# A global spectral filter and a squared-ReLU FFN on one core: the stages B and Y of each batch moved by a slot

## The chip, the cores and the metric

The kernel runs on one core of one Trainium2 chip, in one launch. The metric is the device time of that launch in microseconds; six runs of the kernel before are given.

A core has TensorE (PE, with its weight loads PEld), VectorE (DVE), ScalarE (ACT), GpSimd (POOL) and SyncE (SP). Matmuls write to PSUM, DVE and ACT read it and write to SBUF. Nearly all transfers of this kernel are issued from SP, in program order. Every engine takes its own instructions in the order in which the program gives them, and waits where an input or a buffer is not ready.

## The reference

Eight batches of 3008 positions and 256 channels are filtered in the frequency domain along the positions, and the result goes through a feed-forward layer token by token:

```python
X = np.fft.rfft(x, axis=1)                       # x: (8, 3008, 256)
Y = X * (filt_r + 1j * filt_i)[None, :, :]       # 1505 frequencies
y = np.fft.irfft(Y, n=3008, axis=1)
h = np.maximum(y.reshape(24064, 256) @ w_in, 0)  # w_in: (256, 2048)
return h * h @ w_out                             # w_out: (2048, 256)
```

Inputs and output are float32; the kernel computes with float16 operands and float32 accumulation.

## The kernel before, in words

**The feed-forward layer** sets the frame. The 24064 tokens are 47 groups of 512, and each group has 8 slots, so there are 47 x 8 slots, and 8 more at the end (line 731). In slot s, with g = s // 8 and k = s % 8, the program issues in this order:

1. `ffn_g1(g, k)` (L560): four matmuls of 512 columns, which give two of the sixteen 128-row tiles of the hidden layer into one of two psH buffers, and ACT's ReLU of them into `h` (L564). A group that spans two batches has more and narrower matmuls.
2. place 0 of the slot: what the plan of the filter puts there.
3. `ffn_g2(g - 1, k)` (L577): eight matmuls of 256 columns on the previous group's `h` into psO. `h` is the stationary operand. For even k they read hidden tiles 0 to 7, which are those of that group's slots 0 to 3, for odd k tiles 8 to 15, those of its slots 4 to 7.
4. place 1 of the slot.
5. `ffn_out`: in every fourth slot (s % 4 == 3) ACT copies psO out (L588) and SP writes it to the output (L603, L605).
6. `ffn_sq(g, k)` (L568): DVE squares what ACT wrote in step 1.

**The filter** of batch b is a two-step Fourier transform, its product and its inverse, spread over the slots of earlier groups so that the batch is ready when its tokens come up. Its units:

- A (16 units, `unit_a`, L346): one matmul of 512 columns into psF, copied by ACT (even) or DVE (odd); each fourth is followed by a write of the chunk to `dU` in DRAM. DVE casts x beforehand (`cast_x`, L338), 4 per batch, from loads of x (`load_x`, L192), two of which wait for the buffers that the first two casts free.
- the read of `dU` back in another layout, in two DMAs (`read_u`, L434) into the single tile `ut`.
- B (12 units, `unit_b`, L437): two matmuls of 256 columns into psF (L443). On DVE the product with the filter (L451, "product" below) and two copies across partition halves (L458, L459), and then, as unit S, the sum (L465), which leaves `yf`.
- P (12 units, `unit_p`): two matmuls of 256 columns from `yf` into psF (L494), copied by ACT (L496). After P 2, 5, 8 and 11 SP writes a part of `dZ` to DRAM (L499).
- the read of `dZ` in a third layout, eight DMAs of 192 KB into four tiles `zt` (`read_z`, L512).
- Y (16 units, `unit_y`, L516): four matmuls of 94 columns from `zt` into psF (L530), copied into the batch's `yt` by ACT for even and by DVE for odd units (L537, L539); the last four of batch 0 all by ACT. `ffn_g1` reads `yt`. Units 0 to 3 give the first 752 tokens of the batch, units 4 to 7 the next 752.

`psF` has two buffers (L157), which go round through all of A, B, P and Y in program order: a unit waits until the unit two before it has been emptied.

The order is written out by hand. `fft_plan(b)` (L608) gives each unit a slot and a place, in slots relative to the batch; `first` (L727) turns them into slots of the program: 0 for batch 1, and 40, 88, 136, 184, 232, 280 for batches 2 to 7. All of these are multiples of 8, so that relative slots 24, 32, 40 and 48 of every batch begin a group. Batch b's first tokens are in the group that begins in relative slot 48 (40 for batch 1). Batch 0, and most of A of batch 1, are done before the slots, and Y 4 to 15 of batch 0 in slots 4 to 23 (L616). A unit S is put beside its B, and a P two slots after its B, in place 1. Relative slots before:

| unit | batch 1 | batches 2 to 7 |
|---|---|---|
| A | 8, 9 (last four) | 6 to 13 |
| read_u | 10 | 14 |
| B 0 to 11 | 14 15 17 18 20 22 23 25 27 28 30 32 | 18 19 21 23 24 26 28 30 31 33 35 37 |
| load_x 0, 1 of the next batch | 22 | 27 |
| cast_x 0 to 3 of the next batch (load_x 2, 3 after the first two) | 27 30 33 36 | 32 35 38 41 |
| read_z | 35 | 40 |
| Y | 39 (four), 40 to 45 (two each) | 44 to 51 (two each) |
| Y 12 to 15 of batch 0 | 17 19 21 23 | |

Of the kernel before, what the change touches and what calls it, by code (L numbers as in the profile page):

```python
# [110 lines left out]
def kernel(  # L111
# [496 lines left out]
    def fft_plan(b):  # L608

        plan = {}  # L610

        def put(r, place, f, *a):
            plan.setdefault((r, place), []).append((f, a))

        if b == 1:
            for n in range(4, 16):  # L616
                put(n if n < 8 else n + 2 if n < 12 else 2 * n - 7, n % 2, unit_y, 0, n)
            for k in range(4):
                put((4, 5, 7, 7)[k], 1, cast_wout, k, nc.vector)
        t0 = 2 if b == 1 else 6  # L620
        for a in range(12 if b == 1 else 0, 16):
            put(t0 + a // 2, a % 2, unit_a, b, a)
        put(10 if b == 1 else 14, 1, read_u, b)
        t0 = 14 if b == 1 else 18
        for p in range(12):
            r = t0 + (18 if b == 1 else 19) * p // 11
            put(r, 0, unit_b, b, p)
            put(r, 0, unit_s, b, p)
            put(r + 2, 1, unit_p, b, p)
        t0 = 35 if b == 1 else 40  # L630
        for c in range(4):
            put(t0, 1, read_z, b, c)
        if b + 1 < B:
            for c in range(2):
                put(t0 - 13, 1, load_x, b + 1, c)
            for c in range(4):
                r = t0 - 8 + 3 * c
                put(r, 1, cast_x, b + 1, c)
                if c < 2:
                    put(r, 1, load_x, b + 1, c + 2)  # L640
        for n in range(16):
            if b == 1:
                put(38 + n // 2 if n > 3 else 39, n % 2, unit_y, b, n)
            else:
                put(44 + n // 2, n % 2, unit_y, b, n)
        return plan

    def run(plan, r, place):
# [77 lines left out]
    for b in range(1, B):  # L726
        first = (b * S // TG) * SLOTS - (48 if b > 1 else 40)  # L727
        for (r, place), w in fft_plan(b).items():
            work[(first + r, place)] = w
# [43 lines left out]
```

## Time and profile before

| | |
|---|---|
| six runs | 795.63 to 798.05 us, median 796.97 |
| the profiled execution | 798.05 us; its span, first to last instruction, is 796.2 |
| granted clock of TensorE | 0.998 of full speed |
| first slot begins | 51.5 us into the span |
| bytes read and written in HBM | 58.12 and 48.23 MB, 134 GB/s over the span |

Times in the views are microseconds from the start of the span. A row of the timeline is one operation of one engine or several of a kind: start, length, engine, line, operation, what it writes and reads with the tile's names, the shapes, how many; in brackets the idle time of that engine before it and what ended it. The matmuls' starts are measured, their ends are modelled: a matmul of 256 columns is shown as 272 ns long, while one starts every 109 ns. A row of the view of waits gives the engine, tile and line that waited, what ended the wait, the total, how often, and the longest. The chain that ended last is followed back from the last instruction, and gives the share of the span that each engine has in it.

### The profile page before, as it was taken

How to read it: one execution, taken by the hardware profiler on the slowest of the kernel's cores; microseconds unless marked ns; L12 is line 12 of the kernel's file. 1: busy time of each engine (PE TensorE's matmuls, PEld its weight loads, DVE VectorE, ACT ScalarE, POOL GpSimd, SP SyncE). 2: the span in 40 equal slices, each digit the busy share in tenths (PEclk: the TensorE clock that was granted, in tenths of full speed). 3: DMA queues.
4: the chain of work that ended last, by engine and by line, in shares of the span. 5: the costliest groups of instructions: out<-in, count | busy, mean ns of one | idle time of the engine just before them, and what ended most of it. 6: DMA issues, size and time to landing. Idle time of an engine off the chain costs nothing.

```text
span 796.2 us, 14801 instructions
## 1 busy us (share of the span) xinstructions
PE 781.4 (98%) x6102; PEld 553.2 (69%) x6102; DVE 552.4 (69%) x898; ACT 555.0 (70%) x708; POOL 24.3 (3%) x27
## 2 busy tenths in 40 slices
PE   8989999999999999999999999999999999999998
PEld 5746767666676677867778676776767667776666
DVE  6946995579755897559965699557995579554342
ACT  3856776767667677767777677676777767766664
POOL 3710000000000000000000000000000000000000
PEclk9999999999999999999999999999999999999999
DMA  9994555346814567055461555525563342511111
GB/s 350 366 264 143 138 157 130 88 137 160 202 53 107 154 167 183 28 162 157 121 183 48 169 156 134 132 68 158 151 175 97 86 141 80 122 50 41 40 41 54
DMA packets 88139, 107.32 MB, mean 135 GB/s; under 512 B 6288, under 2 KB 78864, under 8 KB 83856
## 3 DMA queue, kind: packets, MB, share of 16 engines
q1 hardware_dynamic: 87864, 106.19, 46.9%
q8 instruction: 48, 0.79, 0.4%
q10 hardware_dynamic: 144, 0.18, 0.1%
q14 instruction: 19, 0.16, 0.1%
q0 software_dynamic: 64, 0.00, 0.0%
HBM read 58.12 MB, written 48.23 MB: 134 GB/s over the span
## 4 chain that ended last, share of the span: by engine, by line
PE 93%; DMA 4%; DVE 1%; ACT 1%; issue 0%; SPq 0%; ACTq 0%; DVEq 0%
PE psO L577 40%; PE psH L560 39%; PE psB L443 3%; PE psA L359 3%; PE psY L530 3%; PE psP L494 2%; DMA zt<-dZ 1%; DMA ut<-dU 1%; PE warm L274 1%; DMA dZ<-ze 1%; PE psf L293 1%; PE psf L296 1%; ACT h L564 1%; DMA dU<-u 0%; PE psP L480 0%; PE psT L420 0%
## 5 line engine op out<-in xcount | busy, mean ns | idle before, releaser
L564 ACT ACTIVATE h<-psH 128x1024 f16<-128x1024 f32 x376 | 385.2, 1025 | 190.5 <-PE psH L560 187.6
L577 PE MATMUL psO<-sWout,h 128*128 128x256 f16 x3008 | 388.6, 272 | 0.0
L560 PE MATMUL psH<-yt,sWin 128*128 128x512 f16 (+7 forms) x1728 | 386.9, 351 | 1.8 <-DVE yt L539 0.8
L577 PEld LDWEIGHTS <-h 128*128 128x128 f16 x3008 | 290.6, 98 | 77.2
L568 DVE TENSOR_TENSOR h<-h 128x1024 f16<-128x1024 f16 x376 | 253.8, 685 | 100.7 <-ACT h L564 99.2
L560 PEld LDWEIGHTS <-sWin 128*128 128x128 f16 x1728 | 159.5, 98 | 101.7 <-issue 3.5
L451 DVE TENSOR_TENSOR prod<-psB,sF 128x1024 f16<-128x1024 f32 x84 | 102.5, 1220 | 6.3 <-PE psB L443 6.0
L539 DVE CAST yt<-psY 128x376 f16<-128x376 f32 x62 | 34.0, 550 | 58.3 <-PE psY L530 58.3
L365 DVE CAST u<-psA 96x512 f16<-96x512 f32 x50 | 34.3, 687 | 47.3 <-PE psA L359 45.1
L496 ACT CAST ze<-psP 128x512 f16<-128x512 f32 x84 | 49.2, 586 | 17.8 <-PE psP L494 15.9
L588 ACT COPY ost<-psO 128x512 f32<-128x512 f32 (+1 forms) x96 | 55.7, 580 | 6.7 <-PE psO L577 5.3
L530 PEld LDWEIGHTS <-zt 112*128 112x128 f16 x512 | 34.9, 98 | 13.1 <-issue 3.2
L530 PE MATMUL psY<-sC,zt 112*128 112x94 f16 x512 | 42.3, 205 | 1.5 <-DMA zt<-dZ 1.2
L465 DVE TENSOR_TENSOR yf<-prod,yf 128x512 f16<-128x512 f16 x84 | 35.7, 425 | 2.9
L443 PE MATMUL psB<-ut,sSB 128*128 128x256 f16 x192 | 36.5, 272 | 0.7 <-DMA ut<-dU 0.6
L359 PE MATMUL psA<-x,sC 94*96 94x512 f16 x96 | 36.6, 382 | 0.0
L443 PEld LDWEIGHTS <-sSB 128*128 128x128 f16 x192 | 18.6, 98 | 21.3 <-issue 2.1
L494 PE MATMUL psP<-yf,sSP 128*128 128x256 f16 x168 | 32.1, 273 | 0.2 <-ACT yt L537 0.2
L537 ACT CAST yt<-psY 128x376 f16<-128x376 f32 x66 | 30.8, 468 | 1.6 <-PE psY L530 1.0
L338 DVE CAST x<-x 94x2048 f16<-94x2048 f32 x24 | 29.2, 1216 | 0.0
L363 ACT CAST u<-psA 96x512 f16<-96x512 f32 x50 | 28.6, 572 | 0.0
L458 DVE COPY yf<-prod 64x512 f16<-64x512 f16 x84 | 24.3, 290 | 2.9
(63 smaller groups left out, 253.1 us busy)
## 6 DMA issues: line engine op xcount, KB each, us to landing
x<-in_x_dram SPq DMA_DIRECT2D x20, 768.0 KB
zt<-dZ SPq DMA_DIRECT2D x64, 192.0 KB
dU<-u SPq DMA_DIRECT2D x28, 384.0 KB
dZ<-ze SPq DMA_DIRECT2D x28, 384.0 KB
out_dram<-ost SPq DMA_DIRECT2D x66, 128.0 KB
out_dram<-ost SPq DMA_DIRECT2D x31, 256.0 KB
ut<-dU SPq DMA_DIRECT2D x7, 1024.0 KB
xw<-in_x_dram SPq DMA_DIRECT2D x4, 1024.0 KB
```

What stands on the lines that cost most here:

```text
L359: nc.tensor.matmul(ps[0:96, :], sSA, x16s[(b, c)][:, m, :], start=True, stop=True)
L443: nc.tensor.matmul(ps[:, i * D:(i + 1) * D], sSB[:, 2 * p + i, :], uts[b][:, 2 * p + i, :], start=True, stop=True)
L451: nc.vector.tensor_mul(out=prod, in0=ps.rearrange("p (a d) -> p a d", d=D).unsqueeze(1).to_broadcast([128, 2, 2, D]), in1=sF[:, :, 2 * p:2 ...
L465: nc.vector.tensor_add(out=yf, in0=prod[:, 0], in1=yf)
L494: nc.tensor.matmul(ps[:, i * D:(i + 1) * D], sSP[:, 2 * p + i, :], yf[:, i, :], start=True, stop=True)
L496: nc.scalar.copy(out=zes[(b, c)][:, 2 * i6:2 * i6 + 2, :], in_=ps.rearrange("p (a d) -> p a d", d=D))
L530: nc.tensor.matmul(ps[:, 94 * jj:94 * jj + 94], zt[:, 4 * (g % 2) + jj, dt * 128:(dt + 1) * 128], sSY, start=True, stop=True)
L560: nc.tensor.matmul(ps[:, i, o:o + n], sWin[:, dt, jt * 128:(jt + 1) * 128], yts[b][:, dt, r:r + n], start=(dt == 0), stop=(dt == 1))
L564: nc.scalar.activation(out=h2[:, 2 * s:2 * s + 2, :], in_=ps, func=AF.Relu)
L568: nc.vector.tensor_mul(out=v, in0=v, in1=v)
L577: nc.tensor.matmul(pso[g][:, t % 2, :], h2s[g][:, jt, t * 128:(t + 1) * 128], sWout[:, jt, :], start=(jt == 0), stop=(jt == NJT - 1))
L588: nc.scalar.copy(out=ost[:, h0:h0 + step, :], in_=pso[g][:, h0:h0 + step, :])
```

## The change

In batches 2 to 7, B takes relative slots 19 to 37 instead of 18 to 37 (P follows its B as before), and Y takes slots 45 to 52 instead of 44 to 51. In batch 1, B ends in slot 31 instead of 32, `read_z` is in slot 34 instead of 35, and with it the loads and casts of x for batch 2 come one slot earlier, since they are counted from it; its Y begins in slot 38, two units in each slot, instead of four units in slot 39. The other reads and writes keep their slots or follow their unit.

| unit | batch 1 after | batches 2 to 7 after |
|---|---|---|
| B 0 to 11 | 14 15 17 18 20 21 23 24 26 27 29 31 | 19 20 22 23 25 27 28 30 32 33 35 37 |
| load_x 0, 1 of the next batch | 21 | 27 |
| cast_x 0 to 3 | 26 29 32 35 | 32 35 38 41 |
| read_z | 34 | 40 |
| Y | 38 to 45 (two each) | 45 to 52 (two each) |

```diff
-        t0 = 14 if b == 1 else 18
+        t0 = 14 if b == 1 else 19
         for p in range(12):
-            r = t0 + (18 if b == 1 else 19) * p // 11
+            r = t0 + (17 if b == 1 else 18) * p // 11
             put(r, 0, unit_b, b, p)
             put(r, 0, unit_s, b, p)
             put(r + 2, 1, unit_p, b, p)
-        t0 = 35 if b == 1 else 40
+        t0 = 34 if b == 1 else 40
         for c in range(4):
             put(t0, 1, read_z, b, c)
...
         for n in range(16):
-            if b == 1:
-                put(38 + n // 2 if n > 3 else 39, n % 2, unit_y, b, n)
-            else:
-                put(44 + n // 2, n % 2, unit_y, b, n)
+            put((38 if b == 1 else 45) + n // 2, n % 2, unit_y, b, n)
```

## The prediction

> **What bounds the kernel now.** I read the page first: busy shares, then the chain that ended last.
>
> ```profile
> span 796.2 us, 14801 instructions
> PE 781.4 (98%) x6102; PEld 553.2 (69%) x6102; DVE 552.4 (69%) x898; ACT 555.0 (70%) x708; POOL 24.3 (3%) x27
> PE 93%; DMA 4%; DVE 1%; ACT 1%; issue 0%; SPq 0%; ACTq 0%; DVEq 0%
> ```
>
> PE is busy 98% of the span and is 93% of the chain, and the change neither adds nor removes a matmul. So only times at which PE stands still can move the end, and a microsecond saved there is a microsecond off the run. Next, PE's waits from the first slot on (51 us):
>
> ```profile
> PE psY L530 <- DMA zt<-dZ: 1.2, 1, 1.2
> PE psH L560 <- DVE yt L539: 0.8, 2, 0.5
> PE psB L443 <- DMA ut<-dU: 0.6, 2, 0.5
> PE psY L530 <- ACT yt L537: 0.3, 1, 0.3
> PE psP L494 <- ACT yt L537: 0.2, 1, 0.2
> ```
>
> This view counts too little: ends of matmuls are modelled, so a wait shorter than a matmul's tail isn't seen. Starts are measured. From the first of a slot's four psH matmuls to the next operation is 0.86 us where nothing waits (642.12 to 642.98, batch 7's first B). The timeline of PE, at the first B of batches 2 to 6 and the first Y of batches 2 and 6:
>
> ```profile
> 164.39 1.03 PE L560 MATMUL psH<-yt,sWin 128*128 128x512 f16 x4
> 165.56 0.38 PE L443 MATMUL psB<-ut,sSB 128*128 128x256 f16 x2 [0.15 <-DMA ut<-dU]
> ...
> 356.52 1.03 PE L560 MATMUL psH<-yt,sWin 128*128 128x512 f16 x4
> 357.57 0.38 PE L443 MATMUL psB<-ut,sSB 128*128 128x256 f16 x2
> ...
> 642.12 1.03 PE L560 MATMUL psH<-yt,sWin 128*128 128x512 f16 x4
> 642.98 0.38 PE L443 MATMUL psB<-ut,sSB 128*128 128x256 f16 x2
> ...
> 597.36 1.03 PE L560 MATMUL psH<-yt,sWin 128*128 128x512 f16 x4
> 598.45 0.33 PE L530 MATMUL psY<-sC,zt 112*128 112x94 f16 x4
> ```
>
> Distances less 0.86: B of batch 2 lost 0.31 us, batch 3 0.62 (260.97 to 262.45), batch 4 0.19, batches 5 and 6 0.20 each, batch 7 none; Y of batch 2 lost 1.34 (215.09 to 217.29), batch 6 0.23. The other first Ys lost nothing. Batch 1's slot of four Ys:
>
> ```profile
> 124.80 0.50 PE L530 MATMUL psY<-sC,zt 112*128 112x94 f16 x8
> 126.44 0.70 PE L530 MATMUL psY<-sC,zt 112*128 112x94 f16 x8 [0.26 <-ACT yt L537]
> 126.98 0.57 PE L560 MATMUL psH<-yt,sWin 128*128 128x448 f16 x3
> 127.86 0.63 PE L560 MATMUL psH<-yt,sWin 128*128 128x64 f16 x5 [0.31 <-DVE yt L539]
> ```
>
> Eight psO matmuls end 0.87 after 125.14, at 126.01; Y 1 starts at 126.44, 0.43 late: its psF bank is the one that ACT is still emptying. Y 3 starts 0.21 late for the same reason (126.82 against 126.44 + 4 x 0.041). After it, psH of slot 40 waits 0.47 for the last Y's copy.
>
> **The unit of work.** From such rows a bare slot takes PE 1.74 us; a B or a P adds 0.22, a Y 0.17. On DVE, starts follow each other by: product 1.26, its three followers 0.30, 0.32, 0.34, cast of x 1.14, square 0.60 (287.80 - 286.54, and on from 290.62 to 293.93). A product starts 0.42 after its B (286.54 - 286.12). A waiting PE starts 0.05 after the release.
>
> **B and its first wait, batches 2 to 7.** The read of ut stays in relative slot 14, B starts in 19 instead of 18. A slot of 1.74 covers every loss seen (at most 0.62): -1.52 (0.31 + 0.62 + 0.19 + 0.20 + 0.20). Left over: between nothing gained, if the read were late by a whole slot, which no batch shows, and 1.52. I take 1.52.
>
> **Y and its first wait, batches 2 to 7.** The reads of zt stay in slot 40, Y starts in 45 instead of 44: 1.74 against losses of 1.34 and 0.23, so -1.57. No transfer is issued in another slot. What Y feeds: psH of slot 48 is the first to read the batch, and needs Y 0 to 3. They are now in 45 and 46; DVE copies the last by 0.75 into slot 47 (rows at 314.25 to 314.80 in a slot begun at 314.05), so 1.3 us are left. Slot 52, then slot 53 empty, then the next batch's A in 54: no bank is asked for twice. ACT copies results out in slots 47 and 51 before and after, beside one Y copy each time. Cost nothing; if DVE ran over a microsecond late there, slot 48 would wait.
>
> The Trainium skill, "DMA: Bandwidth & Descriptors", section "Anatomy of one DMA", fits a transfer as about 2.0 us plus bytes over 436 GB/s, for the GpSimd path. For one 192 KB zt read that is an estimate of 2.45 us, landing near 214.3 for the one issued at 211.87, before PE wanted it, and the later Y would win nothing: the sum would be 1.57 worse, 797.0. The trace has 5.42 us from that issue to the Y that waited, and eight such reads in flight; the row decides.
>
> **B's own spacing, batches 2 to 7.** Twelve Bs in 18 slots instead of 19, ending in the same slot 37. DVE is the thin place. Over 283.4 to 301.3 (slots 29 to 37 of batch 3) it was busy 17.18 of 17.90 us. What waits for DVE there is the last P, in slot 39:
>
> ```profile
> 303.78 0.42 DVE L465 TENSOR_TENSOR yf<-prod,yf 128x512 f16<-128x512 f16 x1
> ...
> 304.81 0.38 PE L494 MATMUL psP<-yf,sSP 128*128 128x256 f16 x2
> ```
>
> yf is done at 304.20, 0.61 before P. Batches 2 to 6 all have 0.60 or 0.61; batch 7, which casts no x, 2.06. B 8 moves from slot 31 to 32, the slot of the first cast. Its product then starts 1.28 into slot 32 (as at 286.54, slot begun at 285.26), and B 9's follows 1.26 + 0.30 + 0.32 + 0.34 + 1.14 + 0.60 = 3.96 later, 5.24 after slot 32 begins. Slots 32 (B, P) and 33 (B) take 2.18 + 1.96, so it starts 1.10 into slot 34; before, 0.42 (293.93 - 293.51). P 8 moved into slot 34 makes that 0.22 longer, so DVE is late by 0.68 - 0.22 = 0.46, and DVE has no idle time from there to P 11. Margin: 0.61 - 0.05 - 0.46 = 0.10. I take 0; bounds: -0.1 (idle PE elsewhere lets DVE catch up) to +0.2 a batch, five batches. B's banks: each B from the second on needs the one before out of psF; pairs 22/23, 27/28 and 32/33 leave about 0.5, as 23/24 and 30/31 did. The writes of dZ after P 2, 5 and 8 pass one group of SP's output writes; all four are wanted by slot 40 only. Cost 0.
>
> **Batch 1.** Gains: the two bank waits of slot 39 go (Y 0, 1 now in slot 38): -0.43 - 0.21. The wait of slot 40 stays: Y 3 still ends slot 39, DVE copies it 0.37 to 0.92 after its start, and psH needs it 0.17 + 0.38 = 0.55 after: 0.92 + 0.05 - 0.55 = 0.42 for 0.47, -0.05.
>
> New in slot 23: it now holds B 6, Y 15 of batch 0 and P 5 (P 5 was in 24). They share two psF banks; P 5 gets B 6's. B's product ends 0.87 + 0.42 + 1.22 = 2.51 into the slot, P comes at 0.87 + 0.22 + 0.87 + 0.17 = 2.13: +0.43 (2.51 + 0.05 - 2.13). Slot 17 has the same crowding, and its P waits 0.38 (82.59). Bounds 0.3 to 0.8, the upper if DVE is late. Slot 21 now has Y 14 and B 5 without a P: nothing.
>
> New in slot 33: B 11 moves from slot 32, the first of an FFN group, to 31, the last. psO of slot 33 reads the square of slot 31 with its seventh matmul, 0.86 + 0.65 = 1.51 into the slot.
>
> ```profile
> 113.15 1.28 DVE L568 TENSOR_TENSOR h<-h 128x1024 f16<-128x1024 f16 x2
> 114.36 1.21 DVE L451 TENSOR_TENSOR prod<-psB,sF 128x1024 f16<-128x1024 f32 x1
> 115.61 0.29 DVE L458 COPY yf<-prod 64x512 f16<-64x512 f16 x1
> 115.91 0.29 DVE L459 COPY yf<-prod 64x512 f16<-64x512 f16 x1
> 116.23 0.42 DVE L465 TENSOR_TENSOR yf<-prod,yf 128x512 f16<-128x512 f16 x1
> 116.57 0.69 DVE L568 TENSOR_TENSOR h<-h 128x1024 f16<-128x1024 f16 x1
> ```
>
> Before, that square is the second of the first row and ends at 114.43, 1.13 into slot 33 (begun at 113.30). One slot earlier, it stands where the last row stands: behind B 11's whole work, ending 117.26 - 115.04 = 2.22 into its slot. So +0.75 (2.22 + 0.05 - 1.51); bounds 0.65 to 0.85 (a weight load, 0.098 in its row, may come on top).
>
> P 11, the dZ write, the zt reads and Y 0 of batch 1 all move one slot earlier together (x loads and casts of batch 2 too, past one group of output writes on SP); P 11 to Y 0 was 8.03 us (116.77 to 124.80) and is again about 8.0. Nothing. If a zt read took the 5.42 of batch 2 against the 3.92 between its issue (120.88) and Y, up to 1.5 would come.
>
> **Sum.** -1.52 - 1.57 - 0.64 - 0.05 + 0.43 + 0.75 = -2.60. The profiled execution took 798.05 (span 796.2 and 1.85 around it), so 795.45, say 795.4. It is the slowest of the six runs shown, 1.08 above their median; against 796.97 this is -0.2%. About 0.2%, 1.6 us, is what a measurement of this kernel can tell from no change: the forecast is faster, at that edge.
>
> **Rivals.**
> 1. *DVE falls behind (slower).* Place: P 11 of batches 2 to 6. From B 0's product to the last yf DVE has 12 Bs, 18 squares and 2 casts. At their full durations (2.22, 0.69, 1.22) these take 41.5; P 11 comes 40.3 after that product (20 slots of 1.74, 12 Bs and 11 Ps of 0.22, and 1.74 - 1.28). Each P 11 would wait 1.2: +6, 801.6. It decides from 0.62 a batch on (3.1 us in five, which puts the run 0.2% above before). Against it: squares and casts start 0.60 and 1.14 before their successors, which makes the 41.5 into 39.7. For it: idle moments of DVE inside the stage cost the rest down to the margin of 0.10.
> 2. *DVE a little late:* 0.1 to 0.3 at each P 11: 796.0 to 797.0, within 0.2%.
> 3. *The reads move the wait:* zt of batch 1 late by up to 1.5, or half of the DMA losses stay because transfers run longer in other executions: 796.5 to 797.2, within 0.2%.
> 4. *Batch 1 costs less:* DVE order in slots 31 to 33 leaves the square in time, or P 5's wait is hidden: 794.3 to 794.9, faster.
>
> **Chances.** The sum as it stands 0.56 (794.9 to 796.0, a little over half of it beyond 0.2%), rival 4 0.15, rivals 2 and 3 0.16, rival 1 0.13. So faster 0.32 + 0.15 = 0.47, within 0.2% 0.24 + 0.16 = 0.40, slower 0.13. Range 794.3 to 797.4: it leaves out rival 1 and little else.
>
> **What would show it.** No loss beyond 0.86 at the first B and first Y of batches 2 to 7; no ACT wait at Y 1 and 3 of batch 1; a psP wait for DVE's product in slot 23; a psO wait for the square in slot 33 (about 0.75), which no row of before has. yf to P 11 near 0.1 in batches 2 to 6: a psP wait for yf there is rival 1 or 2. If DMA still stands in PE's waits at psB or psY, the step on the reads was wrong.

## The result and the profile after

| | before | after |
|---|---|---|
| median | 796.78 us (40 runs) | 794.24 us (18 runs) |
| ratio, with its 95% interval | | 0.9972 (0.9961 to 0.9982) |
| profiled execution; its span | 798.05; 796.2 | 793.13; 791.3 |
| first slot begins | 51.52 | 49.25 |
| first psH to last psO matmul (the slots' part) | 741.00 | 738.44 |

Faster by 0.28%, as forecast; the two medians alone would give 0.32%. The slots' part fell by 2.56 us between the two profiled executions; the sum had said 2.60. The median lies 1.2 us below the predicted 795.4 and 0.06 us below the low end of the range, and that difference is not in the slots.

The page after, its span, its busy shares and its chain by engine:

```profile
span 791.3 us, 14799 instructions
PE 779.2 (98%) x6102; PEld 552.6 (70%) x6102; DVE 550.4 (70%) x898; ACT 555.1 (70%) x708; POOL 24.4 (3%) x27
...
PE 93%; DVE 4%; ACT 1%; DMA 1%; issue 0%; ACTq 0%; DVEq 0%
```

PE is still the bound. In the chain, DMA and DVE have changed places: 4% and 1% before, 1% and 4% now. PE's waits after 60 us:

```profile
PE psO L577 <- DVE h L568: 0.6, 1, 0.6
PE psP L494 <- DVE prod L451: 0.3, 1, 0.3
PE psP L494 <- ACT yt L537: 0.2, 1, 0.2
PE psH L560 <- DVE yt L539: 0.2, 1, 0.2
```

No DMA stands there any more. The two uppermost are the two waits that batch 1 was to get. The first B and the first Y of batch 2, in the timeline of PE:

```profile
164.33 1.03 PE L560 MATMUL psH<-yt,sWin 128*128 128x512 f16 x4
165.19 0.38 PE L443 MATMUL psB<-ut,sSB 128*128 128x256 f16 x2
...
214.72 1.03 PE L560 MATMUL psH<-yt,sWin 128*128 128x512 f16 x4
215.58 0.33 PE L530 MATMUL psY<-sC,zt 112*128 112x94 f16 x4
```

Both distances are 0.86, nothing lost; before they were 1.17 and 2.20. The Y of batch 2 before, the largest single loss of the sum:

```profile
215.09 1.03 PE L560 MATMUL psH<-yt,sWin 128*128 128x512 f16 x4
217.29 0.33 PE L530 MATMUL psY<-sC,zt 112*128 112x94 f16 x4 [1.17 <-DMA zt<-dZ]
```

The other batches are as batch 2 after the change. What batch 1 pays, in the timelines of PE and DVE:

```profile
92.13 1.23 DVE L451 TENSOR_TENSOR prod<-psB,sF 128x1024 f16<-128x1024 f32 x1
...
92.80 0.33 PE L530 MATMUL psY<-sC,zt 112*128 112x94 f16 x4
...
93.41 0.38 PE L494 MATMUL psP<-yf,sSP 128*128 128x256 f16 x2 [0.27 <-DVE prod L451]
...
112.30 0.82 PE L577 MATMUL psO<-sWout,h 128*128 128x256 f16 x6
113.71 0.39 PE L577 MATMUL psO<-sWout,h 128*128 128x256 f16 x2 [0.59 <-DVE h L568]
...
112.97 0.68 DVE L568 TENSOR_TENSOR h<-h 128x1024 f16<-128x1024 f16 x1
```

In slot 23 P 5 would have started at 92.97 (four Ys of 0.041 after 92.80) and waits until B 6's product has left the bank, at 93.36: 0.44 lost. In slot 33 psO stops after six of its eight matmuls: the seventh was due at 112.95 (six times 0.109), its square ends at 113.65, it starts at 113.71: 0.76 lost.

### The profile page after: what moved, and what is told of

The parts are those of the page before. It is cut to its first block, busy times and chain, and to the rows that moved or that the text cites. A ratio compares the mean times of both kernels' runs of the same rounds, so it can differ in the third digit from the quotient of the medians.

```text
span 791.3 us, 14799 instructions
## 1 busy us (share of the span) xinstructions
PE 779.2 (98%) x6102; PEld 552.6 (70%) x6102; DVE 550.4 (70%) x898; ACT 555.1 (70%) x708; POOL 24.4 (3%) x27
## 4 chain that ended last, share of the span: by engine, by line
PE 93%; DVE 4%; ACT 1%; DMA 1%; issue 0%; ACTq 0%; DVEq 0%
PE psO L577 40%; PE psH L560 39%; PE psA L359 3%; PE psY L530 3%; PE psB L443 2%; PE psP L494 2%; DVE prod L451 1%; PE warm L274 1%; DVE h L568 1%; PE psf L293 1%; PE psf L296 1%; ACT h L564 1%; DMA zt<-dZ 0%; PE psP L480 0%; PE psT L420 0%; DVE prods L451 0%
```

## The experiments

Ten other kernels, and the two compared once more. The table gives the slots' part of the profiled execution, which matmul starts measure to a few hundredths; the time is given, with its 95% interval, for kernels that ran several times beside the kernel before.

| kernel | slots' part | ratio to before |
|---|---|---|
| before; again | 741.00; 740.45 | |
| only Y, batches 2 to 7 | 740.01 | 0.9999 (0.9986 to 1.0011) |
| only B, batches 2 to 7 | 738.47 | 0.9990 (0.9978 to 1.0002) |
| only batch 1 | 740.29 | 1.0009 (0.9995 to 1.0022) |
| B and Y of batches 2 to 7 | 737.97 | 0.9967 (0.9954 to 0.9981) |
| the change; again | 738.44; 738.47 | 0.9972 (0.9961 to 0.9982); 0.9978 (0.9965 to 0.9992) |
| one slot earlier instead | 760.76 | |
| the change, one more copy on DVE | 739.89 | |
| batch 1 mended, first try | 740.54 | 1.0025 (1.0012 to 1.0037) |
| loads mended | 737.72 | 0.9964 (0.9947 to 0.9980) |
| only the Y units mended | 737.49 | 0.9961 (0.9948 to 0.9974) |
| cast mended too | 736.55 | 0.9964 (0.9948 to 0.9981) |

### The parts, one by one

Only Y of batches 2 to 7:

```diff
-                put(44 + n // 2, n % 2, unit_y, b, n)
+                put(45 + n // 2, n % 2, unit_y, b, n)
```

> Only Y of batches 2 to 7 starts a slot later (45 for 44); B and batch 1 as before. Theory (waits): from the first psH matmul to the last psO matmul it was 741.00 us before (51.52 to 792.51) and 738.44 after; the two waits for zt (1.34 in batch 2, 0.23 in batch 6) cannot be in it, the waits for ut (about 0.2 to 0.6 at the first B of batches 2 to 6) stay, so 739.2 to 739.9 there, and 0.5 to 1.6 us off the run's time. Rival (the front): the profiles also differ by 2.27 us ahead of the first slot; if the change caused that, it needs the whole change, and this part alone moves the time by under 0.5.

The first Ys lost nothing, the first Bs 0.13, 0.75, 0.05, 0.39, 0.34 and 0.42. The slots' part was 740.01, just above the expected 739.2 to 739.9, and the time did not move: the expected 0.5 to 1.6 us did not show, though the interval reaches to 1.1 us faster. The loss at zt was overrated. Where Y keeps its slot it was 0.64 in the second profile of before, 0.51 in the kernel with only B moved and 0.50 in the one with only batch 1 changed; the 1.57 of the first profile was the odd one, through batch 2's 1.34.

Only B and P of batches 2 to 7:

```diff
-        t0 = 14 if b == 1 else 18
+        t0 = 14 if b == 1 else 19
-            r = t0 + (18 if b == 1 else 19) * p // 11
+            r = t0 + (18 if b == 1 else 18) * p // 11
```

> Only B and P of batches 2 to 7 start a slot later (B 19 to 37), Y and batch 1 as before. Theory: no loss at the first B, yf ready 0.12 us before the last P of batches 2 to 6 (0.61 before) and no wait there; first Ys may still lose (0 to 1.5 in all). From the first to the last slot 738.5 to 739.8; time 1.0 to 2.0 less. Rival (DVE falls behind): psP waits for yf at the last P in some of the five batches. Rival (the front): under 0.5 off.

738.47, at the low end of what was expected (738.5 to 739.8); no loss at a first B, no wait at a last P, 0.26 and 0.25 at the first Y of batches 2 and 6. The time fell by 0.1%, with an interval from 0.2% faster to no change: 0.8 us where 1.0 to 2.0 were expected, less than the slots' part says, and not clear of noise.

Only batch 1:

```diff
-            r = t0 + (18 if b == 1 else 19) * p // 11
+            r = t0 + (17 if b == 1 else 19) * p // 11
-        t0 = 35 if b == 1 else 40
+        t0 = 34 if b == 1 else 40
-            if b == 1:
-                put(38 + n // 2 if n > 3 else 39, n % 2, unit_y, b, n)
-            else:
-                put(44 + n // 2, n % 2, unit_y, b, n)
+            put((38 if b == 1 else 44) + n // 2, n % 2, unit_y, b, n)
```

> Only batch 1 is changed. Theory: this part loses: waits of 0.43 in slot 23 and 0.76 in slot 33 come, 0.64 in slot 39 goes and 0.1 in slot 40, so +0.45; from the first to the last slot 741 plus 0.45 less what the ut and zt waits of this execution differ by; time +0.1 to +0.9. If it comes out faster than before by more than 0.5, batch 1 carries part of the gain and the sum of waits is wrong there.

The waits are those of the whole change: 0.44 in slot 23, 0.76 in slot 33, 0.39 in slot 40. The time is 0.1% up, with an interval on both sides of none. This part brings nothing and, by its waits, costs 0.48 (0.44 + 0.76 for 0.43 + 0.21 and 0.08 of slot 40's).

Batches 2 to 7 without batch 1:

```diff
-        t0 = 14 if b == 1 else 18
+        t0 = 14 if b == 1 else 19
-            r = t0 + (18 if b == 1 else 19) * p // 11
+            r = t0 + (18 if b == 1 else 18) * p // 11
-                put(44 + n // 2, n % 2, unit_y, b, n)
+                put(45 + n // 2, n % 2, unit_y, b, n)
```

> The change without its part on batch 1. Theory: all ut and zt waits of batches 2 to 7 gone, batch 1's 0.43 + 0.21 + 0.47 of before there, from the first to the last slot 737.9 to 738.1 (741.00 - 3.09), which is 0.4 to 0.5 below the whole change; time about 3 us below before, 793.7 where before is 796.8. Rival (the parts need each other): no more than the whole change's 2.5.

737.97 of 737.9 to 738.1 expected: 0.47 to 0.50 below the whole change, which is batch 1's bill. The gain is all in the later batches, and the parts do not need each other. The time is 0.33% below before; the interval covers the whole change's too.

### How early is too early

```diff
-        t0 = 14 if b == 1 else 18
+        t0 = 14 if b == 1 else 17
-            r = t0 + (18 if b == 1 else 19) * p // 11
+            r = t0 + (18 if b == 1 else 20) * p // 11
-                put(44 + n // 2, n % 2, unit_y, b, n)
+                put(43 + n // 2, n % 2, unit_y, b, n)
```

> The kernel before with B of batches 2 to 7 starting a slot earlier (17 for 18) and Y a slot earlier (43 for 44). Theory (the transfers set it): the first Bs lose 1.74 more each, 1.7 to 2.4 in each of six batches, the first Ys 1.0 to 3.1 each, together 17 to 25 us; the start of these Bs and Ys then gives the landing of ut and zt, 3.3 to 3.9 us after the issue of the last read that they need. Rival (a fixed transfer time of 2.0 us plus bytes over 436 GB/s, 2.45 for zt): the first Ys of most batches lose under 0.5.

PE's waits after 60 us in this kernel:

```profile
PE psB L443 <- DMA ut<-dU: 11.0, 6, 2.2
PE psY L530 <- DMA zt<-dZ: 8.2, 6, 1.9
```

By starts, the six Bs lost 1.74 to 2.41, 11.96 in all, and the six Ys 1.02 to 2.04, 9.22 in all; the slots' part grew by 19.8 (21.18 less the 3.09 of before, and 1.7 because TensorE ran at half clock from 263.7 to 267.1, after the longest of these waits). All twelve now wait, so their starts give the landing: ut 3.56 to 3.91 us after the issue of its first read, zt 3.41 to 4.45 after that of the second. In the changed kernel PE comes 5.1 to 5.3 and 5.0 to 5.9 after them, so the slot won leaves over a microsecond spare. Batch 2's zt, 5.42 in the profile of before, is 3.85 here: a single late transfer. Against that one, the 5.86 that batch 2 has after the change would leave 0.4.

The Trainium skill, "DMA: Bandwidth & Descriptors", section "Anatomy of one DMA", gives an estimate of 2.45 us for one such zt read (2.0 plus 192 KB at 436 GB/s, for another issue path). The measured 3.41 to 4.45, with eight reads in flight, is 1 to 2 us more, and it is what counts: by the page's estimate the six first Ys would have lost at most 0.6 each and 1.4 in all, for the 9.22 measured.

### How thin DVE is

In the changed kernel, one of B 10's copies is made twice in batches 2 to 7:

```diff
             nc.vector.tensor_copy(out=yf[64:128], in_=prod[0:64, 1])
+            if b > 1 and p == 10:
+                nc.vector.tensor_copy(out=yf[0:64], in_=prod[64:128, 1])
```

> The changed kernel with one copy of 0.30 us more on DVE (the first of B 10's two copies is made twice, the result is the same) in batches 2 to 7. Theory: the last P of batches 2 to 6 has 0.12 us between yf and its start, 0.05 of it the release, so each waits 0.30 - 0.07 = 0.23; batch 7, with 2.05, waits nothing. Five waits of about 0.23 at psP L494, 1.1 to 1.2 us in all. If DVE has slack that the view doesn't show, no wait.

The last sum and the last P of batch 3, in the changed kernel and then with the copy:

```profile
300.21 0.42 DVE L465 TENSOR_TENSOR yf<-prod,yf 128x512 f16<-128x512 f16 x1
...
300.76 0.38 PE L494 MATMUL psP<-yf,sSP 128*128 128x256 f16 x2
```

```profile
302.33 1.04 PE L579 MATMUL psO<-sWout,h 128*128 128x256 f16 x8
303.48 0.39 PE L496 MATMUL psP<-yf,sSP 128*128 128x256 f16 x2
...
303.00 0.43 DVE L467 TENSOR_TENSOR yf<-prod,yf 128x512 f16<-128x512 f16 x1
```

In the changed kernel yf is done 0.13 before P starts. With the copy it ends at 303.43 and P, due at 303.20 (0.87 after the first of eight psO matmuls), starts at 303.48, 0.28 late. All five batches lost 0.28, batch 7 nothing; the slots' part grew by 1.45. The margin was as thin as worked out, 0.07 after the release, and 0.35 rather than 0.30 came to it from the copy. The view of waits shows none of these five: they are shorter than the modelled tail of a matmul.

### A version without batch 1's waits

Four units go to other slots:

```diff
-                put(n if n < 8 else n + 2 if n < 12 else 2 * n - 7, n % 2, unit_y, 0, n)
+                put(n if n < 8 else n + 2 if n < 12 else (16, 19, 21, 25)[n - 12], n % 2, unit_y, 0, n)
-                r = t0 - 8 + 3 * c
+                r = (26, 32, 34, 36)[c] if b == 1 else t0 - 8 + 3 * c
-            put((38 if b == 1 else 45) + n // 2, n % 2, unit_y, b, n)
+            put((38 if b == 1 else 45) + n // 2, 0 if b == 1 and n == 3 else n % 2, unit_y, b, n)
```

> The changed kernel with four units of batches 0 to 2 in other slots: Y 12 and Y 15 of batch 0 in slots 16 and 25 for 17 and 23, the casts of x for batch 2 in 26, 32, 34, 36 for 26, 29, 32, 35, and Y 3 of batch 1 in place 0 of slot 39. Theory: waits in slots 17 (0.38), 23 (0.44), 33 (0.76) and 40 (0.39) go, about 1.9 us; from the first to the last slot 736.5 to 736.8; time 1.5 to 2 us below the changed kernel run beside it, 4 to 4.5 below before. If a wait only moves (DVE is 17 of 18 us busy there), slots 18 to 36 show another psP, psB or psO wait of 0.3 or more.

A miss: all four waits went, and the kernel became 0.25% slower than before. The whole loss is in slots 38 and 39, in the timeline of PE and SP:

```profile
121.75 1.03 PE L560 MATMUL psH<-yt,sWin 128*128 128x512 f16 x4
124.99 0.34 PE L530 MATMUL psY<-sC,zt 112*128 112x94 f16 x4 [2.22 <-DMA zt<-dZ]
...
126.43 1.91 PE L560 MATMUL psH<-yt,sWin 128*128 128x512 f16 x4
...
115.27 0.32 SPq L192 DMA_DIRECT2D x<-in_x_dram  x1
115.69 0.38 SPq L499 DMA_DIRECT2D dZ<-ze  x1
116.17 8.85 SPq L512 DMA_DIRECT2D zt<-dZ  x8
```

Y 0 of batch 1 lost 2.38, and the matmuls behind it 1.66 more. The later second cast had moved the load of x that follows it, 768 KB, to just ahead of the last dZ write. The zt reads wait for that write; the second of them was issued at 121.93, 6.2 us after the write, against 3.1 in the changed kernel (118.03 after 114.97). That the load is the cause is tested by moving it alone behind the reads, and the last cast, which needs it, to slot 41:

```diff
-                r = (26, 32, 34, 36)[c] if b == 1 else t0 - 8 + 3 * c
+                r = (26, 32, 34, 41)[c] if b == 1 else t0 - 8 + 3 * c
-                    put(r, 1, load_x, b + 1, c + 2)
+                    put(36 if b == 1 and c else r, 1, load_x, b + 1, c + 2)
```

> The mended kernel once more, with the last load of x for batch 2 in slot 36, behind the reads of zt on SP, and its cast in slot 41; the first casts stay in 26, 32, 34. Theory (the load of 768 KB ahead of the last dZ write made that write land 6.2 us after its issue, 3.1 in the changed kernel): the dZ write lands in about 3.1 again, Y 0 of batch 1 loses under 0.3 in slot 38, and slots 17, 23, 33 and 40 lose nothing, so 736.4 to 736.9 from the first to the last slot, 1.6 to 2.0 less than the changed kernel, and 4 us (0.5%) below before. Rival (the casts or the units of batch 0 did it, by way of DVE or the psF banks): Y 0 still loses 1 us or more.

Confirmed: the write landed in 3.0 (116.40 to 119.41), Y 0 lost nothing. But slots 42 and 43 lost 0.60 and 0.59, which was not expected, and the part was 737.72. DVE's timeline there:

```profile
129.49 0.68 DVE L568 TENSOR_TENSOR h<-h 128x1024 f16<-128x1024 f16 x1
131.52 1.22 DVE L338 CAST x<-x 94x2048 f16<-94x2048 f32 x1 [1.35 <-DMA x<-in_x_dram]
132.66 0.54 DVE L539 CAST yt<-psY 128x376 f16<-128x376 f32 x1
```

The cast stood at the head of DVE's queue until x came, 8.4 us after its issue at 123.08, and a Y's copy stood behind it. Beside this kernel one ran with the first and the last line of the first try only, so without any change to loads and casts:

> The changed kernel with only Y 12, Y 15 of batch 0 and Y 3 of batch 1 moved (16, 25 and place 0 of 39), loads and casts as in the changed kernel. Theory: slots 17, 23 and 40 lose nothing, slot 33 its 0.76, Y 0 of batch 1 under 0.3 in slot 38: 737.2 to 737.5 from the first to the last slot, about 1.2 below the changed kernel and 3.7 below before.

737.49; slots 17, 23 and 40 lost nothing (0.05 in 40), slot 33 0.94 instead of 0.76. Last, the mended loads with the cast four slots later:

```diff
-                r = (26, 32, 34, 41)[c] if b == 1 else t0 - 8 + 3 * c
+                r = (26, 32, 34, 45)[c] if b == 1 else t0 - 8 + 3 * c
```

> The kernel with mended loads, and the last cast of x for batch 2 in slot 45 instead of 41. Theory (in slot 41 the cast stood at the head of DVE's queue until x landed, and the copy of a Y and two squares behind it came late, which cost 0.6 in each of slots 42 and 43): x has landed by slot 43, the cast waits for nothing, both waits go, and from the first to the last slot 736.4 to 736.7 is left; time 0.5% below before, 1.8 us below the changed kernel. Rival (ACT's own load there is too high): the psY waits of slots 42 and 43 stay.

736.55, and both waits gone: from slot 9 on PE loses 0.05 us. This is 1.9 below the change and 4.45 below before in the slots' part (3.90 below its second profile), 0.36% below before in time. All three kernels that work lie 0.1% below the change; their intervals overlap with its own, so that they beat it is shown by the slots' part, not by the times.

### The front

> The changed kernel again, beside the mended one on the same chip. Theory: 0.2 to 0.4% below before; the front before the first slot differs from the first profile of it (49.25) by up to 2 us with no change in the program, since it does not come from the change; from the first to the last slot 738.3 to 738.7. Rival (the front): 49.2 to 49.3 again, with 51.5 in kernels that lack the change.

> The kernel before, once more. From the first to the last slot 739.5 to 741.5, by how late ut and zt come in this execution. Theory on the front: the first slot begins at 49 to 52.5 us, by how long PE waits for the cast of x and at which clock it goes on, as in the kernels with and without the change (48.8 to 52.4 in ten profiles); a front of 51 or more would still allow that the change shortens it.

Changed kernel again: front 49.44, part 738.47. Before again: front 51.29, part 740.45. That alone would fit a change that shortens the front. But the kernel with only batch 1 changed has 48.78, and those with batch 1 changed and more (the extra copy, the three mended, the Y units) have 51.0 to 52.9, like those that lack it (50.7 to 52.4). What divides them is the clock. Three stretches around the wait for the cast of x, in the profile of before and in that of after (the column after POOL is the granted clock):

```profile
40.00:43.20 3.20, 0.60 (x5) 0.25 (x4) 0.00 (x0) 1.01 (x1) 1.31 (x2) 1.00 0.91 277
43.20:46.60 3.40, 3.40 (x10) 1.62 (x9) 1.31 (x2) 1.16 (x2) 0.71 (x1) 0.50 0.37 106
46.60:50.00 3.40, 3.40 (x21) 2.04 (x20) 1.79 (x3) 2.07 (x3) 0.00 (x0) 1.00 0.99 286
```

```profile
40.00:43.20 3.20, 1.77 (x10) 0.98 (x10) 0.00 (x0) 1.64 (x3) 2.03 (x2) 1.00 0.87 264
43.20:46.60 3.40, 3.40 (x16) 1.92 (x16) 2.07 (x3) 1.81 (x3) 0.00 (x0) 1.00 0.71 176
46.60:50.00 3.40, 2.90 (x31) 1.83 (x30) 2.77 (x5) 1.65 (x4) 0.00 (x0) 1.00 1.09 328
```

In the same 3.4 us PE did 10 matmuls at half clock and 16 at full. Between 42.5 and 46.5 us the mean clock was 1.00 in the three profiles with a short front (48.8 to 49.4) and 0.50 to 0.69 in the eleven others. Half clock comes in stretches of 3.4 us: the front is 48.8 to 49.4 with none, 50.7 to 52.2 with one, 52.4 and 52.9 with two. So the 2.27 us between the fronts of the first two profiles come from the clock and the length of one wait in that execution, and not from anything that the change moves.

## Why the prediction was right, and where it was off

- **Reading of the losses.** Right, and worked from starts: all losses at ut and zt are gone, in every batch. As sizes, ut's 1.52 is typical (1.36, 1.87 and 2.07 in three other profiles), zt's 1.57 is not (0.50 to 0.64). One profile could not tell the two apart: batch 2's 1.34 stands in it like any other row.
- **Batch 1's new waits.** 0.43 and 0.75 predicted, 0.44 and 0.76 measured; slot 39's two went, slot 40's fell from 0.47 to 0.39 (0.42 predicted).
- **DVE's margin at P 11.** 0.10 predicted, about 0.07 in the trace after (0.13 less the release of 0.05), and the added copy's wait of 0.28 fits it; no wait. Rivals 1 and 2 fell on that, but the added copy shows how near they were: 0.3 us of DVE work there costs 1.4 us of the run.
- **Rival 3.** No wait moved to another place: batch 1's Y lost nothing, and the slot gained exceeds the landings of the kernel one slot earlier by over a microsecond. Rival 4 did not happen: both waits came in full.
- **The step that failed** is the last of the sum, "The profiled execution took 798.05 ..., so 795.45". It took the sum from the slowest run's own time as if its surplus lay in the waits removed. 2.27 us of the difference to the next profile lay in the front, 51.52 against 49.25, where the change moves nothing. The same sum from the median would have been 796.97 - 2.60 = 794.37, 0.13 from what was measured. That closeness is partly luck. With the waits of before's second profile the sum is 2.0, as the slots' parts say (740.45 - 738.47 = 1.98). Where the change ran again beside before, runs at the same granted clock, 1.000, have median spans of 791.4 (9 of 12 runs) and 793.1 (7 of 19), 1.7 apart, while the medians of all these runs lie 2.8 apart.

The kernels with B alone and Y alone showed less in time (0.8 and 0.0 us) than in the slots' part (2.0 to 2.5 and 0.4 to 1.0). The granted clock of each of these runs explains most of that: one stretch of 3.4 us at half clock takes 0.002 off the mean of a run, and only 1 of 12 runs of either kernel was at 1.000, against 14 of the 35 runs of before beside them. Among the runs at 0.998 the median span is 795.0 before (6 runs), 793.3 with B alone (8) and 794.4 with Y alone (6): 1.7 and 0.6 less.

What stays open is why runs at full clock are so much more frequent with some kernels (9 of 12 with the change run again, 1 of 12 with Y alone), though the program up to the first slot is the same. No run here decides whether the change has a part in it.

## What to carry to other kernels

Where one engine is busy to 98%, list its late starts against the spacing of its own matmuls, not against idle time, and price a change of order as the sum of those that go and those that come. Put the sum on the median, ask first which part of the profiled run lies in stretches that the change does not touch, and compare times among runs of the same granted clock. When a unit is moved, look at what its place releases: a cast moved three slots freed a buffer later, that put a load ahead of a write on which PE waited, and it cost twice what the move had won.

## What the runs showed of the hardware that was not expected

- Half clock came with short waits. In the front, one wait of PE, for the cast of x, lasted 1.6 to 2.9 us (start to start, less the 0.22 of the matmul before). In eleven of fourteen profiles a stretch at half clock began during that wait or up to 1.5 us behind it; in three, with waits of 1.6 to 1.8, none did. With the first mended kernel it happened in the middle of the run, after the wait of 2.22:

```profile
124.00:126.00 2.00, 1.01 (x12) 0.93 (x13) 0.00 (x0) 0.47 (x1) 0.00 (x0) 0.99 1.02 199
126.00:128.00 2.00, 2.00 (x10) 0.97 (x9) 1.15 (x2) 0.00 (x0) 0.00 (x0) 0.50 1.07 193
```

  The wait itself cost 2.38, the half clock after it 1.66. What fits all fourteen profiles is a grid with cells of 3.413 us: counted from the start of the first stretch at full clock, the clock changes only after a whole number of them. After each of the sixteen cells in which PE was idle for 1.92 us or more (by the modelled ends) the next ran at half clock, after none with 1.66 or less; of the four between, those with 1.74 and 1.76 were followed by half clock, two with 1.87 were not. Two cells and the ones behind them, in the kernel with only Y moved (1.74 idle) and in the one with only batch 1 changed (1.61):

```profile
38.39:41.80 3.41, 1.67 (x12) 0.93 (x10) 1.75 (x2) 1.99 (x2) 1.20 (x2) 1.00 1.03 346
41.80:45.21 3.41, 2.68 (x7) 1.34 (x7) 0.35 (x1) 1.20 (x3) 1.66 (x2) 0.50 0.53 159
```

```profile
39.55:42.96 3.41, 1.80 (x10) 0.97 (x9) 0.00 (x0) 1.76 (x3) 2.03 (x2) 1.00 0.91 269
42.96:46.37 3.41, 3.41 (x17) 1.94 (x16) 2.20 (x3) 1.82 (x4) 0.00 (x0) 1.00 0.63 164
```

  So the idle time within one cell fits, and the length of one wait does not: in the front, an idle gap of 1.43 us was not followed by half clock in after, where it lies across two cells (1.46 idle in the fuller one), and was in the kernel one slot earlier, where two shorter waits share its cell (1.76 idle). This is read off the profiles; no run moved a wait along the grid to test it.

  The Trainium skill, "TensorE: Matmul & The Clock Gate", part 1, has a free-running window of about 3.4 us for this, and the 3.413 us here agree. Its later rule, "no PE-idle gaps >~3.4µs", is too lax for this case, where 1.74 us of idle PE in one cell was enough.
- In batch 1, 3.1 us passed in the changed kernel from the issue of the last write of dZ (384 KB) to the issue of the read that waits for it, 3.0 with the loads mended, and 6.2 in the first mended kernel, with a load of 768 KB issued 0.4 us ahead of the write on the same queue. In batches 2 to 7 of the changed kernel, where writes of results are issued in between, it was 2.9 to 3.7.
